# A statically scheduled transformer block: value weights by row blocks, one tile's layernorm sums on ScalarE, an earlier MLP weight load, a refitted cost model and a new ordering rule

## The chip, the cores and the metric

One core of a Trainium2 chip. The metric is the device time of one execution in microseconds (us). Each kernel is run several times; most runs of one kernel agree within 0.3%, and where they don't I say so. A profile records one execution; its span, from the first to the last instruction, is some 1.7 us shorter than the time.

PE is the matmul engine (TensorE), PEld its weight loads, DVE is VectorE, ACT is ScalarE, POOL is GpSimd, SP is SyncE. SP issues nearly all DMAs here, in order. A DMA *lands* when its completion is signalled; an engine *evicts* a result when it copies it out of PSUM. All runs here but one are in the fast state (granted clock 0.994 to 1.0); the slow one is e12's profiled run.

## The reference

Layernorm of x, then two branches that read the same normalised x, added to x. Shapes: S = 2048 rows, D = 640, 32 heads of 20, F = 1536, bf16.

```python
xn = layernorm(x)
q, k, v = split_heads(xn @ wqkv)
phi = lambda t: concat(softmax(t @ w_phi), softmax(-(t @ w_phi)))   # 20 -> 40 features per head
kv, z = phi(k)^T @ v, sum_s phi(k)
attn = (phi(q) @ kv) / (phi(q) @ z + 1e-6) @ wo
glu  = (silu(xn @ w1) * (xn @ w3)) @ w2
out  = x + attn + glu
```

## The kernel before

The rows are 16 tiles of 128. The program is not written in its final order. It is a set of *streams* (layernorms, transposes, keys and values, queries, MLP, output, ...). At build time, a list scheduler picks the next step again and again, with a cost model that guesses when each engine and each DMA will be done. The order it finds is fixed into the program; at run time the engines only wait on semaphores. A change of one guessed latency can therefore reorder everything after it.

The parts that matter here:

```python
# the cost model's DMA part (in commit); "T" marks a DMA that transposes
self.free[o.eng] = t + 0.45
if "T" == o.part:
    self.free[o.eng] = t + max(1.3, o.cost / 150e3)
self.bus = max(self.bus, t + 0.5) + o.cost / (280e3 if o.part else 305e3)
o.end = self.bus + (1.6 if t < 3.5 else 2.6)
# ... cut ...
def first_loads():
    load_x(0, 1)                      # and x tile 1 from ACT's queue
    for a in (0, 320):                # wv in two column halves
        P.dma("SP", wv[:, :, a:a + 320], wqkv_t[:, :, 2 * D + a:2 * D + a + 320])
        load_x(2 + a // 320, 3 + a // 320)
    w13(0, 512)                       # MLP columns 0-511 of w1 and w3
    # ... phi, wqkT for the keys, x tiles 4-11; columns 512-1023 only once xnT of tile 7 is issued
# ... cut ...
def ln_sums(t, q):                    # DVE: two of these per tile, then one aggregate
    P.op("DVE", "bn_stats", ...)
# ... cut: the choice of the next step, among all streams ...
if any(o.eng == "PE" for o in ops):
    at = max(P.ready(ops), P.free["PE"] + 0.15)
    if i == MLPS and P.free["DVE"] > P.free["PE"] + LAG:
        rank = n
# ... the smallest (at, rank) wins, so rank decides among steps that are ready
```

Names in the traces: `xnT` is the normalised x, transposed; `PS` is PSUM; `w_s` covers w1, w3 and w2; `wqkT` are the transposed query and key weights, which are multiplied ("folded") with the block-diagonal `BDc`; `eqt`/`EqT` are the query features of a tile and their transpose, made by a DMA; `KVc` is the kv state; `oT` is the attention output, transposed by a DMA as well.

The softmax here doesn't subtract the row's maximum and nothing guards it: scores larger than these inputs give would overflow.

Of the kernel before, what the change touches and what calls it, by code (L numbers as in the profile page):

```python
# [3 lines left out]
ACT = mybir.ActivationFunctionType  # L4
# [5 lines left out]
D = 640  # L10
# [33 lines left out]
class _Program:  # L44
# [123 lines left out]
    def commit(self, ops):  # L168
        for o in ops:
            o.idx = len(self.ops)  # L170
            o.deps = self.find_deps(o)
            t = self.free[o.eng]
            for d in o.deps:
                t = max(t, d.end + 0.07)
            o.start = t
            if o.dma:
                self.free[o.eng] = t + 0.45
                if "T" == o.part:
                    self.free[o.eng] = t + max(1.3, o.cost / 150e3)
                self.bus = max(self.bus, t + 0.5) + o.cost / (280e3 if o.part else 305e3)  # L180
                o.end = self.bus + (1.6 if t < 3.5 else 2.6)
            else:
                o.end = t + o.cost
                self.free[o.eng] = o.end
            self.ops.append(o)
            if o.eng == "POOL" and not o.dma:
                self.pool = o
            for g in o.reads:
                if isinstance(g, tuple):
                    self.bank.setdefault(g, {})[o.eng] = o  # L190
                else:
                    self.last_r.setdefault(g, {})[("dma", o.idx) if o.dma else o.eng] = o
            for g in o.writes:
                if isinstance(g, tuple):
                    self.bank.setdefault(g, {})[o.eng] = o
                else:
                    self.last_w[g] = o
                    self.last_r.pop(g, None)
# [45 lines left out]
def bass_parallel_sum__linear_kernel_hedgehog__glu_gated_swiglu__prompt_kernel(  # L244
# [10 lines left out]
):  # L255
    bf = DT.bfloat16
    LAG = 4.0
    AHEAD = 2
    PACE = 2.2
    f32 = DT.float32  # L260
# [25 lines left out]
    rstd = new("rstd", [128, T, 8], f32)  # L286
    mhalf = new("mhalf", [128, 4], f32)
    warm = new("warm", [128, 8], f32)
    g_s = new("g_s", [128, 2, H], f32)
    FM = new("FM", [128, 6, 3], bf)  # L290
    S64 = new("S64", [128, 3, 72], f32)
# [114 lines left out]
    def load_x(a, b):  # L406
        P.dma("SP", x_tok[:, a:b, :], x_t[:, a:b, :])

    def first_loads():
        load_x(0, 1)  # L410
        o = P.dma("ACT", x_tok[:, 1:2, :], x_t[:, 1:2, :])
        o.reads = P.regions(zero[:])
        for a in (0, 320):
            P.dma("SP", wv[:, :, a:a + 320], wqkv_t[:, :, 2 * D + a:2 * D + a + 320])
            load_x(2 + a // 320, 3 + a // 320)
        w13(0, 512)
        P.dma("SP", phi_s[:], phi_t)
        P.dma("SP", wqkT[:, DC:2 * DC, :], A_wqkv[:, D:2 * D], True)
        load_x(4, 8)
        load_x(8, 12)  # L420


    def consts():
# [21 lines left out]
    def ln_rstd(t0, n):  # L445
        for t in range(t0, t0 + n):
            o, i = mv[:, t, 0:2], bst[:, t, 0:15]
            P.op("DVE", "bn_aggr", [o], [i], (o, i), cost=0.15)
        m, v, r, z = mv[:, t0:t0 + n, 0], mv[:, t0:t0 + n, 1], rstd[:, t0:t0 + n, 0], rstd[:, t0:t0 + n, 1]
        P.op("POOL", "tensor_tensor", [r], [v, mhalf[:, 0:n]], (r, v, mhalf[:, 0:n], ALU.pow),  # L450
             cost=0.6)
        if t0 >= 4:
            P.op("POOL", "tensor_scalar_mul", [z], [m], (z, m, -1.0), cost=0.25)
            P.op("POOL", "tensor_tensor", [z], [z, r], (z, z, r, ALU.mult), cost=0.25)

    def ln_stats(t0, n):
        for t in range(t0, t0 + n):
# [50 lines left out]
    def proj(t, w, k):  # L508
        for q in range(2):
            for i in range(DC):  # L510
                mm(bank(k + q, 320), xnT[:, i, t * 128:(t + 1) * 128],
                   w[:, i, 320 * q:320 * q + 320], i == 0, i == DC - 1)

    def v_half(t, q, k):
        for i in range(DC):
            mm(bank(k, 320), xnT[:, i, t * 128:(t + 1) * 128], wv[:, i, 320 * q:320 * q + 320],
               i == 0, i == DC - 1)
        evac(v2[:, t, 336 * q:336 * q + 336].rearrange("p (h c) -> p h c", c=21)[:, :, 0:DH],
             bank(k, 320).rearrange("p (h c) -> p h c", c=DH))

    def v_tile(t, k):
        proj(t, wv, k)
# [29 lines left out]
    def normalise(e, c, n):  # L552
        s, r = S64[:, nnorm[0] % 3, 0:c * n], rS64[:, nnorm[0] % 3, 0:c * n]
        nnorm[0] += 1
        P.op("DVE", "tensor_reduce", [s], [e], (s, e, AX.X, ALU.add), cost=0.12 + free(e) / 960)
        P.op("DVE", "reciprocal", [r], [s], (r, s), cost=0.65)
        r = r.rearrange("p (c n) -> p c n", n=n)
        for a, b in ((0, c // 2), (c // 2, c)):
            ev = e[:, a:b, :, :]
            tt("POOL", ev, ev, r[:, a:b, :].unsqueeze(3).to_broadcast([128, b - a, n, DH]), ALU.mult)  # L560
# [89 lines left out]

    def norms():
        yield lambda: (memset("DVE", zero[:], 0.0), memset("DVE", warm[:], 0.0), first_loads(), consts())
        for t in range(4):
            yield lambda t=t: ln_sums(t, 0)
            if t == 1:
                for c, lo, hi in ((1, 0, 256), (2, 256, D)):
                    yield lambda lo=lo, hi=hi: ln_apply(0, lo, hi)
                    done["first"] = c
                done["ln"] = 1
            elif t:  # L660
                yield lambda t=t: ln_apply(t - 1)
                done["ln"] = t
            yield lambda t=t: (ln_sums(t, 1), ln_rstd(t, 1))
        yield lambda: ln_apply(3)
        done["ln"] = 4
        yield block_diag
        todo = []
        for t in range(4, T + 2, 2):
            if t == T or t > done["k"] + 8 or t == 12 and done["w"] < 8:
                for u in todo:  # L670
                    yield lambda u=u: ln_apply(u)
                    done["ln"] = u + 1
                todo = []
            if t == T:
                break
            while t > done["k"] + 8 or t == 12 and done["w"] < 8:
                yield None
            yield lambda t=t: ln_stats(t, 2)
            for u in todo:
                yield lambda u=u: ln_apply(u)  # L680
                done["ln"] = u + 1
            todo = [t, t + 1]
        yield consts_late
# [3 lines left out]
            yield lambda dc=dc: fold_mm(1, dc, banks(2))  # L687
        done["f"] += 1

    done["w"] = 4  # L690

    def k_norms():
        for t in range(T):
# [54 lines left out]
    def loads():  # L748
        while done["t"] < 4:
            yield None  # L750
        for t in range(4, T):
            while done["ln"] <= t:
                yield None
            yield lambda t=t: P.dma("SP", xnT[:, :, t * 128:(t + 1) * 128], x_tok[:, t, :], True)
            done["t"] = t + 1
            if t == 7:
                yield lambda: (w13(512, 1024), load_x(12, 16))
                done["w"] = 8
            if t == 9:
                yield lambda: w13(1024, 1536)  # L760
                done["w"] = 12
                yield lambda: P.dma("SP", wqkT[:, 0:DC, :], A_wqkv[:, 0:D], True)
                done["f"] = 2

    def attention():
# [4 lines left out]
        for t in range(4):  # L770
            while done["t"] <= t:
                yield None
            for q in range(2):
                yield lambda t=t, q=q: v_half(t, q, banks(1))
        while done["f"] < 1:
# [44 lines left out]
    def outs():  # L820
        for t in range(T):
            while done["o"] <= t or done["h"] <= t // 4:
# [2 lines left out]

    streams = [norms(), transposes(), fold_k(), attention(), k_norms(), loads(), queries(), q_norms(),
               q_transposes(), o_transposes(), mlps(), outs()]
    MLPS = 10
    URGENT = {0: 4.0, 4: 4.0, 7: 4.0, 8: 4.0, 9: 4.0}
    n = len(streams)  # L830
    heads, alive = [None] * n, [True] * n
    while any(alive):
        best = None
        for i in range(n):
            if heads[i] is None and alive[i]:
                s = next(streams[i], StopIteration)
                if s is StopIteration:
                    alive[i] = False
                else:
                    heads[i] = s  # L840
            if heads[i] is None:
                continue
            save = nmlp[0], nnorm[0], len(finish)
            ops = P.step(heads[i])
            after = nmlp[0], nnorm[0], finish[save[2]:]
            nmlp[0], nnorm[0] = save[:2]
            del finish[save[2]:]
            rank = i
            if any(o.eng == "PE" for o in ops):
                at = max(P.ready(ops), P.free["PE"] + 0.15)  # L850
                if i == MLPS and P.free["DVE"] > P.free["PE"] + LAG:
                    rank = n
            else:
                at = P.start_of(ops[0])
                if i in URGENT:
                    now, mine = P.free["PE"], P.free[ops[0].eng]
                    if at <= max(now, mine) + 0.3 and at < now + URGENT[i]:
                        at = now + 0.1 - URGENT[i]
            if best is None or (round(at, 2), rank) < best[:2]:
                best = (round(at, 2), rank, i, ops, after)  # L860
# [69 lines left out]
```

## Time and profile before

272.03 us median of three runs (271.89 to 272.31). From the page of the profile (busy time and share of the span by engine, then busy tenths in 40 slices of the span, then the chain that ended last):

```profile
span 270.6 us, 4817 instructions
PE 264.2 (98%) x1951; PEld 162.6 (60%) x1951; DVE 184.0 (68%) x308; ACT 101.9 (38%) x218; POOL 99.3 (37%) x108
...
PE   8899989999999999999999999999999999999996
...
DMA  7981799850000396463856636150726300031211
...
PE 86%; ACT 6%; DMA 5%; SPq 2%; issue 0%; DVE 0%
```

PE is busy nearly all the time, and nearly all of that is work at full rate. So the ceiling for any change that removes no matmul is the time that PE waits. I cut the span into three segments: the start (up to the first MLP matmul), the middle (from there to the first matmul of the kv sum), and the late part (to the end of PE's work: kv, queries, output). From the view of stretches; the columns are the stretch, its length, the busy time of PE, PEld, DVE, ACT and POOL, the granted clock, the DMA share and GB/s:

```profile
0.00:14.50 14.50, 12.21 (x75) 6.61 (x76) 7.75 (x22) 5.66 (x12) 6.00 (x21) 1.00 0.99 252
14.50:85.75 71.25, 69.89 (x472) 43.14 (x470) 61.01 (x99) 49.13 (x75) 51.26 (x55) 1.00 0.50 116
85.75:268.27 182.52, 182.05 (x1407) 112.80 (x1405) 114.93 (x188) 47.15 (x131) 42.08 (x33) 1.00 0.40 86
...
20.00:25.00 5.00, 5.00 (x36) 3.42 (x35) 4.86 (x14) 3.13 (x5) 2.25 (x6) 1.00 0.00 0
```

The middle has 1.36 us without PE work, the start 2.3 us, the late part 0.5 us. The last line shows the stretch in which the DMA queue does nothing. PE's timeline of the start (start, duration, engine, operation, output<-inputs, shapes, count, and in brackets the idle time before and what ended it):

```profile
6.41 1.09 PE L102 MATMUL PS<-wv,xnT 128*128 128x320 bf16 x5
7.93 0.85 PE L102 MATMUL PS<-wv,xnT 128*128 128x320 bf16 x5 [0.43 <-DMA wv<-in_A_wqkv_dram]
8.62 0.44 PE L102 MATMUL PS<-ident,x_tok 128*128 128x128 bf16 x5
9.58 0.96 PE L102 MATMUL PS<-wv,xnT 128*128 128x320 bf16 x5 [0.53 <-ACT xnT L102]
...
12.10 0.44 PE L102 MATMUL PS<-ident,x_tok 128*128 128x128 bf16 x5
12.38 2.28 PE L102 MATMUL PS<-wv,xnT 128*128 128x320 bf16 x15
...
14.50 2.32 PE L102 MATMUL PS<-xnT,w_s 128*128 128x512 bf16 x10
```

`ident,x_tok` are the five transposes of a tile, `wv,xnT` its values. And of the middle, the two places where PE waits:

```profile
40.02 1.52 PE L102 MATMUL PS<-Wkp,xnT 128*128 128x320 bf16 x10 [0.70 <-DMA xnT<-x_tok]
...
48.42 0.47 PE L102 MATMUL PS<-BDc,wqkT 128*128 128x140 bf16 x6 [0.65 <-DMA wqkT<-in_A_wqkv_dram]
```

A bracket gives idle time after a modelled end of the matmul before. The start-to-start excess over the matmul's own rate is larger: 0.87 and 0.82 us. I use the latter below for PE's waits.

### The profile page before, as it was taken

How to read it: one execution, taken by the hardware profiler on the slowest of the kernel's cores; microseconds unless marked ns; L12 is line 12 of the kernel's file. 1: busy time of each engine (PE TensorE's matmuls, PEld its weight loads, DVE VectorE, ACT ScalarE, POOL GpSimd, SP SyncE). 2: the span in 40 equal slices, each digit the busy share in tenths (PEclk: the TensorE clock that was granted, in tenths of full speed). 3: DMA queues.
4: the chain of work that ended last, by engine and by line, in shares of the span. 5: the costliest groups of instructions: out<-in, count | busy, mean ns of one | idle time of the engine just before them, and what ended most of it. 6: DMA issues, size and time to landing. Idle time of an engine off the chain costs nothing.

```text
span 270.6 us, 4817 instructions
## 1 busy us (share of the span) xinstructions
PE 264.2 (98%) x1951; PEld 162.6 (60%) x1951; DVE 184.0 (68%) x308; ACT 101.9 (38%) x218; POOL 99.3 (37%) x108
## 2 busy tenths in 40 slices
PE   8899989999999999999999999999999999999996
PEld 3556666577446846476756565657564444677773
DVE  4569689799896399959779766749577766311112
ACT  3467997687431455405233224043312222000000
POOL 3314288689998082704555221303330000000000
PEclk9999999999999999999999999999999999999999
DMA  7981799850000396463856636150726300031211
GB/s 209 288 235 24 185 269 290 107 150 2 0 0 2 105 290 129 59 126 65 173 78 145 140 66 126 27 126 0 127 57 126 51 0 0 0 94 54 81 43 48
DMA packets 63366, 27.73 MB, mean 102 GB/s; under 512 B 49904, under 2 KB 63344, under 8 KB 63344
## 3 DMA queue, kind: packets, MB, share of 16 engines
q1 hardware_dynamic: 63200, 27.26, 44.9%
q8 instruction: 15, 0.25, 0.4%
q10 hardware_dynamic: 144, 0.16, 0.2%
q14 instruction: 7, 0.06, 0.1%
HBM read 12.81 MB, written 2.62 MB: 57 GB/s over the span
## 4 chain that ended last, share of the span: by engine, by line
PE 86%; ACT 6%; DMA 5%; SPq 2%; issue 0%; DVE 0%
PE PS L102 86%; DMA wqkT<-in_A_wqkv_dram 3%; ACT ekt L102 3%; DMA wv<-in_A_wqkv_dram 2%; SPq L114 2%; ACT x_tok L102 1%; ACT v L102 1%; ACT eqt L102 0%; ACT th L102 0%; DVE xres L102 0%; ACT xnT L102 0%
## 5 line engine op out<-in xcount | busy, mean ns | idle before, releaser
L102 PE MATMUL PS<-xnT,w_s 128*128 128x512 bf16 x480 | 107.0, 379 | 0.5 <-ACT eqt L102 0.5
L102 PEld LDWEIGHTS PS<-xnT,w_s 128*128 128x128 bf16 x480 | 46.4, 98 | 53.4 <-ACT eqt L102 0.8
L102 POOL TENSOR_TENSOR eqt<-eqt,rS 128x600 bf16<-128x600 bf16 (+1 forms) x32 | 40.9, 1305 | 75.5 <-DVE rS L102 75.5
L102 ACT ACTIVATE th<-PS 128x512 f32<-128x512 f32 x48 | 28.7, 597 | 75.6 <-PE PS L102 75.6
L102 PE MATMUL PS<-w_s,hT 128*128 128x320 bf16 (+2 forms) x384 | 54.9, 299 | 0.0
L102 DVE SCALAR_TENSOR_TENSOR t<-th,PS 128x512 bf16<-128x512 f32 x48 | 32.4, 676 | 29.6 <-ACT th L102 29.6
L102 PEld LDWEIGHTS PS<-w_s,hT 128*128 128x128 bf16 x384 | 37.1, 98 | 15.1
L102 POOL TENSOR_TENSOR ekt<-ekt,rS 128x640 bf16<-128x640 bf16 x32 | 39.6, 1274 | 8.4 <-DVE rS L102 8.4
L102 ACT ACTIVATE eqt<-PS 128x240 bf16<-128x240 f32 (+1 forms) x96 | 26.7, 348 | 35.0 <-PE PS L102 34.5
L102 DVE TENSOR_TENSOR xres<-PS,xres 128x640 bf16<-128x640 f32 (+2 forms) x17 | 13.4, 786 | 37.2 <-PE PS L102 37.1
L102 DVE SCALAR_TENSOR_TENSOR hT<-t,PS 128x512 bf16<-128x512 bf16 x48 | 33.0, 687 | 1.7
L102 PE MATMUL PS<-wv,xnT 128*128 128x320 bf16 x160 | 25.0, 299 | 1.1 <-ACT xnT L102 0.5
L102 DVE TENSOR_REDUCE S<-eqt 128x66 f32<-128x1320 bf16 x16 | 24.1, 1509 | 2.6 <-ACT eqt L102 2.6
L102 ACT ACTIVATE ekt<-PS 128x640 bf16<-128x640 f32 x32 | 22.3, 702 | 8.6 <-PE PS L102 8.0
L102 PE MATMUL PS<-Wkp,xnT 128*128 128x320 bf16 x160 | 23.9, 299 | 0.7 <-DMA xnT<-x_tok 0.7
L102 PE MATMUL PS<-wo_s,oT 128*128 128x320 bf16 (+2 forms) x160 | 24.5, 299 | 0.0
L102 PE MATMUL PS<-Wqp,xnT 128*128 128x360 bf16 (+1 forms) x160 | 23.7, 299 | 0.0
L102 DVE TENSOR_REDUCE S<-ekt 128x64 f32<-128x1280 bf16 x16 | 23.1, 1447 | 0.0
L102 PEld LDWEIGHTS PS<-wv,xnT 128*128 128x128 bf16 x160 | 15.0, 98 | 8.3 <-ACT xnT L102 1.7
L102 PEld LDWEIGHTS PS<-Wkp,xnT 128*128 128x128 bf16 x160 | 15.4, 98 | 7.2 <-ACT ekt L102 1.0
L102 PEld LDWEIGHTS PS<-Wqp,xnT 128*128 128x128 bf16 x160 | 15.2, 98 | 6.8
L102 PEld LDWEIGHTS PS<-wo_s,oT 128*128 128x128 bf16 x160 | 15.1, 98 | 6.4
(48 smaller groups left out, 157.1 us busy)
## 6 DMA issues: line engine op xcount, KB each, us to landing
w_s<-in_B_w_dram SPq DMA_DIRECT2D x6, 640.0 KB, 6.7
xres<-in_A_x_dram SPq DMA_DIRECT2D x16, 160.0 KB, 2.5
out_dram<-xres SPq DMA_DIRECT2D x15, 160.0 KB, 1.9
x_tok<-in_A_x_dram SPq DMA_DIRECT2D x3, 640.0 KB, 6.4
w_s<-in_B_w_dram SPq DMA_DIRECT2D x1, 1920.0 KB, 8.5
wv<-in_A_wqkv_dram SPq DMA_DIRECT2D x2, 400.0 KB, 4.9
wo_s<-in_A_wo_dram SPq DMA_DIRECT2D x1, 800.0 KB, 4.9
x_tok<-in_A_x_dram SPq DMA_DIRECT2D x3, 160.0 KB, 4.3
```

The source lines that it names most:

```text
L102: o = _Op(eng, lambda: m(*args, **kw), r, w, cost)
L114: o = _Op(eng, lambda: m(out, in_), self.regions(in_), self.regions(out), nbytes, True)
```

## The change

The intent: fill the idle stretches of PE. wv comes in row blocks, so that tile 0 can begin on the first rows and use both column halves; the sums of layernorm tile 1 are made by ACT's accumulators while DVE does tile 0; MLP columns 512-1023 are loaded in the idle stretch of the DMA queue instead of in front of x of tiles 12-15; keys yield to MLP blocks when ACT is behind; and the cost model is fitted to measured latencies. The core of the diff:

```diff
+                turn = "T" == o.part
+                self.free[o.eng] = t + (max(1.28, o.cost / 120e3) if turn else 0.46)
+                rate = (280e3 if o.cost < 300e3 else 235e3) if turn else 330e3 if t < 4.5 else 285e3
+                self.bus = max(self.bus, t + 0.5) + o.cost / rate
+                o.end = self.bus + (1.6 if turn else 1.5 if t < 4.5 else 1.9)
 ... (replaces the five lines shown above)
-        for a in (0, 320):
-            P.dma("SP", wv[:, :, a:a + 320], wqkv_t[:, :, 2 * D + a:2 * D + a + 320])
-            load_x(2 + a // 320, 3 + a // 320)
+        for t, a, b in ((2, 0, 2), (3, 2, DC)):
+            P.dma("SP", wv[:, a:b, :], wqkv_t[:, a:b, 2 * D:3 * D])
+            load_x(t, t + 1)
 ...
         load_x(8, 12)
+        w13(512, 1024)
 ...
+    def act_sums(t):
+        i = x_tok[:, t, :]
+        for f, c in ((ACT.Copy, 0), (ACT.Square, 1)):
+            a = sums[:, c, 0:1]
+            P.op("ACT", "activation", [xres[:, c, :], a], [i], (xres[:, c, :], i, f), dict(accum_out=a), ...)
 ... (mean and variance from the sums by four small DVE operations; the power on POOL as before)
+            if t == 0:
+                for lo, hi in ((0, 3), (3, 4), (4, DC)):
+                    yield lambda lo=lo, hi=hi: v_first(0, lo, hi)
+                continue
 ...
-                yield lambda: (w13(512, 1024), load_x(12, 16))
-                done["w"] = 8
+                yield lambda: load_x(12, 16)
 ...
+                if i == ATTN and not done["kv"] and P.free["ACT"] > P.free["PE"] + ALAG:    # ALAG = 3.0
+                    rank = n + 1
 ... (layernorms run 7 instead of 8 tiles ahead of the keys; eight MLP blocks are at hand from the beginning; the guessed cost of a reciprocal on DVE falls from 0.65 to 0.56 us)
```

More of the change, by code (lines that the diff above doesn't have):

```diff
@@ L176, in commit @@
             if o.dma:
-                self.free[o.eng] = t + 0.45
-                if "T" == o.part:
-                    self.free[o.eng] = t + max(1.3, o.cost / 150e3)
-                self.bus = max(self.bus, t + 0.5) + o.cost / (280e3 if o.part else 305e3)
-                o.end = self.bus + (1.6 if t < 3.5 else 2.6)
+                turn = "T" == o.part
[3 more added lines that the diff above has]
+                o.end = self.bus + (1.6 if turn else 1.5 if t < 4.5 else 1.9)
             else:
@@ L257, in bass_parallel_sum__linear_kernel_hedgehog__glu_gated_swiglu__prompt_kernel @@
     LAG = 4.0
+    ALAG = 3.0
+    LEAD = 7
     AHEAD = 2
@@ L288, in bass_parallel_sum__linear_kernel_hedgehog__glu_gated_swiglu__prompt_kernel @@
     warm = new("warm", [128, 8], f32)
+    sums = new("sums", [128, 4, 8], f32)
     g_s = new("g_s", [128, 2, H], f32)
@@ L454, in ln_rstd, with small, act_mean, act_rstd @@
             P.op("POOL", "tensor_tensor", [z], [z, r], (z, z, r, ALU.mult), cost=0.25)
+    def act_sums(t):
+        i = x_tok[:, t, :]
+        for f, c in ((ACT.Copy, 0), (ACT.Square, 1)):
+            a = sums[:, c, 0:1]
+            P.op("ACT", "activation", [xres[:, c, :], a], [i], (xres[:, c, :], i, f), dict(accum_out=a),
+                 cost=0.2 + D / 960)
+    def small(o, i, a, f, b=None, g=None):
+        r = [x for x in (i, a, b) if hasattr(x, "ap")]
+        P.op("DVE", "tensor_scalar", [o], r, (o, i, a, b, f) + (() if g is None else (g,)), cost=0.13)
+    def act_mean(t):
+        m, n, q = mv[:, t, 0:1], sums[:, 2, 0:1], sums[:, 3, 0:1]
+        small(m, sums[:, 0, 0:1], 1.0 / D, ALU.mult)
+        small(n, sums[:, 0, 0:1], -1.0 / D, ALU.mult)
+        small(q, n, m, ALU.mult, EPS, ALU.add)
+    def act_rstd(t):
+        v, r = mv[:, t, 1:2], rstd[:, t, 0:1]
+        small(v, sums[:, 1, 0:1], 1.0 / D, ALU.mult, sums[:, 3, 0:1], ALU.add)
+        P.op("POOL", "tensor_tensor", [r], [v, mhalf[:, 0:1]], (r, v, mhalf[:, 0:1], ALU.pow), cost=0.6)
     def ln_stats(t0, n):
@@ L512, in proj, with v_out @@
                    w[:, i, 320 * q:320 * q + 320], i == 0, i == DC - 1)
+    def v_out(t, q, k):
+        evac(v2[:, t, 336 * q:336 * q + 336].rearrange("p (h c) -> p h c", c=21)[:, :, 0:DH],
+             bank(k, 320).rearrange("p (h c) -> p h c", c=DH))
     def v_half(t, q, k):
@@ L517, in v_half, with v_first @@
                i == 0, i == DC - 1)
-        evac(v2[:, t, 336 * q:336 * q + 336].rearrange("p (h c) -> p h c", c=21)[:, :, 0:DH],
-             bank(k, 320).rearrange("p (h c) -> p h c", c=DH))
+        v_out(t, q, k)
+    def v_first(k, lo, hi):
+        for i in range(lo, hi):
+            for q in range(2):
+                mm(bank(k + q, 320), xnT[:, i, 0:128], wv[:, i, 320 * q:320 * q + 320], i == 0, i == DC - 1)
+        if hi == DC:
+            v_out(0, 0, k)
+            v_out(0, 1, k + 1)
     def v_tile(t, k):
@@ L555, in normalise @@
         P.op("DVE", "tensor_reduce", [s], [e], (s, e, AX.X, ALU.add), cost=0.12 + free(e) / 960)
-        P.op("DVE", "reciprocal", [r], [s], (r, s), cost=0.65)
+        P.op("DVE", "reciprocal", [r], [s], (r, s), cost=0.56)
         r = r.rearrange("p (c n) -> p c n", n=n)
@@ L652, in norms @@
         yield lambda: (memset("DVE", zero[:], 0.0), memset("DVE", warm[:], 0.0), first_loads(), consts())
-        for t in range(4):
-            yield lambda t=t: ln_sums(t, 0)
-            if t == 1:
-                for c, lo, hi in ((1, 0, 256), (2, 256, D)):
-                    yield lambda lo=lo, hi=hi: ln_apply(0, lo, hi)
-                    done["first"] = c
-                done["ln"] = 1
-            elif t:
-                yield lambda t=t: ln_apply(t - 1)
-                done["ln"] = t
+        yield lambda: act_sums(1)
+        yield lambda: ln_stats(0, 1)
+        yield lambda: act_mean(1)
+        for c, lo, hi in ((1, 0, 256), (2, 256, D)):
+            yield lambda lo=lo, hi=hi: ln_apply(0, lo, hi)
+            done["first"] = c
+        done["ln"] = 1
+        yield lambda: act_rstd(1)
+        for t in range(2, 4):
+            yield lambda t=t: ln_sums(t, 0)
+            yield lambda t=t: ln_apply(t - 1)
+            done["ln"] = t
             yield lambda t=t: (ln_sums(t, 1), ln_rstd(t, 1))
@@ L668, in norms @@
         for t in range(4, T + 2, 2):
-            if t == T or t > done["k"] + 8 or t == 12 and done["w"] < 8:
+            if t == T or t > done["k"] + LEAD or t == 12 and done["t"] < 8:
                 for u in todo:
@@ L675, in norms @@
                 break
-            while t > done["k"] + 8 or t == 12 and done["w"] < 8:
+            while t > done["k"] + LEAD or t == 12 and done["t"] < 8:
                 yield None
@@ L688, in fold_k @@
         done["f"] += 1
-    done["w"] = 4
+    done["w"] = 8
     def k_norms():
@@ L827, in bass_parallel_sum__linear_kernel_hedgehog__glu_gated_swiglu__prompt_kernel @@
                q_transposes(), o_transposes(), mlps(), outs()]
-    MLPS = 10
+    MLPS, ATTN = 10, 3
     URGENT = {0: 4.0, 4: 4.0, 7: 4.0, 8: 4.0, 9: 4.0}
```

## The prediction

> **What bounds it now.** TensorE. The page gives PE busy 264.2 of 270.6 us (98%), DVE 68%, ACT 38%; the chain that ended last is 86% PE. In the PE timeline the 480 MLP matmuls of 512 columns start 217.5 ns apart, the 320-column ones 136 ns. The Trainium skill ("TensorE: Matmul & The Clock Gate", section "Wait — 56ns, not 53.3ns?") gives N / 2.4 GHz + about 2.5 ns, 215.8 and 135.8: the trace agrees, so nearly the whole span is at the engine's floor, and no matmul is removed. Start-to-start excesses over 60 ns sum to 7.0 us, 1.7 of it the half-rate warm-up. Recoverable are about 5.3 us:
>
> 1. Start, 5.1 to 13 us: 2.7 us. PE waits 0.43 us for the second wv half (landed 7.88), 0.53 for xnT of tile 1, and works in pieces; v of tiles 0-3 ends at 14.5.
> 2. 39.0 us: 0.87 us. xnT of tile 8, issued at 31.5 behind two w loads and x 12-15 (issued 29.7 to 30.9), landed at 39.88.
> 3. 47.4 us: 0.82 us. Transposed wqkT landed at 48.29, same queue. (0.64 us at 110.7 us, on ACT eqt, is not addressed.)
>
> Even a perfect result is near 266.7 us, 1.95% better.
>
> **What the change does.**
> - wv by rows: same bytes and place in the queue, rows of 1280 B instead of 640. All of wv should land where the second half does, 7.4 to 7.8 us; tile 0 starts with two row blocks. Small gain.
> - ACT sums for tile 1: a 640-wide eviction took 0.70 us, so I estimate 0.7 to 0.85 us for each of two. x tile 1 landed at 3.56 and ACT is idle until 5.97, so they end about 5.3. DVE loses two bn_stats (0.5 us each) and an aggregate (0.22) and gains four small operations (estimate 0.1 us each). Tile 1's apply moves from 7.1 to about 6.6, tile 3's from 11.3 to about 10.2; v of tiles 0-3 should end at 12.8 to 13.5: 1.0 to 1.7 us gained. The first MLP needs w3, landed at 12.08, so it can use this.
> - MLP columns 512-1023: 1.3 MB move from 29.7 us, where they delay tile 8, into 20 to 25 us, where the DMA share is 0.00. At about 300 GB/s they fit just before the xnT transposes of 24.5 us. Later loads land several us earlier; stalls 2 and 3 should go: 1.7 us.
> - Eight instead of four MLP chunks are available early, and keys yield when ACT lags over 3 us (ACT is fully busy from 25 to 40 us). This moves work; I count no gain beyond stall 2.
> - The altered cost model reorders everything statically. I allow 0.2 to 0.5 us of new stalls.
>
> **Sum.** 1.4 + 1.7 - 0.2 = 2.9 us, all on PE, the critical path: about 269.1; I say 269.0 us, 267.5 to 271.0. Faster by over 2% (under 266.6) 0.04, within 2% 0.94, slower by over 2% 0.02.
>
> **What would show it.** PE busy stays near 263 to 264 us while span falls to about 267.6. v of tile 3 ends before 13.5 us; no 0.4 us wait on wv; two 640-wide ACT activations between 3.6 and 5.4 us; w columns 512-1023 issued near 14 us, landed before 25; no PE wait on xnT<-x_tok near 39 us nor on wqkT near 48 us; from 68 us on all merely shifted.
>
> **What would make it wrong.** A second activation table load for Square (the first took 1.28 us); the accumulating activations running into tile 0's evictions; DVE's small operations waiting on ACT and holding back tile 0's apply; the early w load delaying the first xnT transposes and so the keys; new stalls from the reordered keys, queries and MLPs, which could eat the whole gain.

## The result, and the profile after

270.76 us median (270.69 to 270.91, four runs), before 272.17 us in all runs together; the ratio is 0.9949, with a 95% interval of 0.9932 to 0.9967. A ratio is the mean time of one kernel's fast runs over that of the other's fast runs of the same rounds, so it is not quite the ratio of the medians. So the change gained 1.4 us where I had forecast 3.0: the right direction and inside the range, but less than half the size.

```profile
span 269.0 us, 4811 instructions
PE 263.8 (98%) x1951; PEld 162.6 (60%) x1951; DVE 183.2 (68%) x305; ACT 107.0 (40%) x226; POOL 99.6 (37%) x108
...
PE   7999999999999999999999999999999999999996
...
DMA  7995798241000683844727325164206142011211
...
PE 93%; DMA 4%; ACT 1%; SPq 1%; DVE 0%; issue 0%
```

The same three segments:

```profile
0.00:13.67 13.67, 11.85 (x76) 6.63 (x76) 7.28 (x23) 7.00 (x16) 5.54 (x20) 1.00 0.95 254
13.67:83.28 69.61, 69.60 (x473) 43.26 (x470) 60.20 (x95) 52.59 (x79) 50.65 (x57) 1.00 0.51 121
83.28:266.67 183.39, 182.38 (x1407) 112.76 (x1405) 115.44 (x188) 47.40 (x131) 43.43 (x33) 1.00 0.38 85
```

Against before, the start is 0.83 us shorter, the middle 1.64 us shorter (PE is busy for all of it now), and the late part is **0.87 us longer**. The sum, 1.60 us, is the difference of the two spans. Both traces have 130 MLP matmuls ahead of the kv sum, so the segments hold the same work.

The start:

```profile
6.46 0.97 PE L102 MATMUL PS<-wv,xnT 128*128 128x320 bf16 x4 [0.20 <-ACT xnT L102]
7.72 0.45 PE L102 MATMUL PS<-wv,xnT 128*128 128x320 bf16 x2 [0.30 <-DMA wv<-in_A_wqkv_dram]
8.01 0.44 PE L102 MATMUL PS<-ident,x_tok 128*128 128x128 bf16 x5
8.28 1.43 PE L102 MATMUL PS<-wv,xnT 128*128 128x320 bf16 x9
...
11.27 0.44 PE L102 MATMUL PS<-ident,x_tok 128*128 128x128 bf16 x5
11.55 2.28 PE L102 MATMUL PS<-wv,xnT 128*128 128x320 bf16 x15
...
13.67 2.32 PE L102 MATMUL PS<-xnT,w_s 128*128 128x512 bf16 x10
```

After 7.72 us PE hardly pauses; before that it does little. The transposes of tile 1 (8.01) stand *behind* the two matmuls that wait for the second row block, although their input was ready at 7.07. The two lines that waited in the middle have no counterpart any more. The late part, where it lost time:

```profile
175.13 2.32 PE L102 MATMUL PS<-xnT,w_s 128*128 128x512 bf16 x10
177.85 0.51 PE L102 MATMUL PS<-KVc,EqT 128*128 128x63 bf16 x11 [0.40 <-DMA EqT<-eqt]
```

PE waits there 0.57 us (start to start) for a transposed query tile, a wait that before did not have. A second new one of 0.30 us stands before the MLP block at 104.78. PE's own line names nothing there, but that of its weight loads does, ACT's eviction of query features:

```profile
104.78 1.84 PEld L102 LDWEIGHTS PS<-xnT,w_s 128*128 128x128 bf16 x10 [0.25 <-ACT eqt L102]
```

So the late part's 0.87 us are 0.57 for a transpose and 0.30 for ACT. Another wait on ACT eqt, of 0.64 us, is in both kernels (110.7 us before, 108.5 after).

### The profile page after: what moved, and what is told of

It reads as the page before. It is cut to its first block, busy times and chain, and to the rows that moved or that the text cites. A ratio compares the mean times of both kernels' runs of the same rounds, so it can differ in the third digit from the quotient of the medians.

```text
span 269.0 us, 4811 instructions
## 1 busy us (share of the span) xinstructions
PE 263.8 (98%) x1951; PEld 162.6 (60%) x1951; DVE 183.2 (68%) x305; ACT 107.0 (40%) x226; POOL 99.6 (37%) x108
## 3 DMA queue, kind: packets, MB, share of 16 engines
q1 hardware_dynamic: 62560, 27.26, 43.5%
## 4 chain that ended last, share of the span: by engine, by line
PE 93%; DMA 4%; ACT 1%; SPq 1%; DVE 0%; issue 0%
PE PS L102 93%; DMA wv<-in_A_wqkv_dram 2%; DMA EqT<-eqt 2%; ACT eqt L102 1%; SPq L114 1%; DVE xres L102 0%
## 5 line engine op out<-in xcount | busy, mean ns | idle before, releaser
L102 PE MATMUL PS<-xnT,w_s 128*128 128x512 bf16 x480 | 108.2, 379 | 0.6 <-ACT eqt L102 0.5
L102 DVE TENSOR_TENSOR xres<-PS,xres 128x640 bf16<-128x640 f32 (+2 forms) x17 | 13.4, 786 | 33.1 <-PE PS L102 33.1
L102 DVE RECIPROCAL rS<-S 128x64 f32<-128x64 f32 (+1 forms) x32 | 17.9, 560 | 1.1
```

What stands on the lines that cost most here:

```text
L102: o = _Op(eng, lambda: m(*args, **kw), r, w, cost)
```

## The experiments

Fifteen runs (e15 is the changed kernel again), all of them correct. Where it helps I give "first MLP" (the end of the start) and "late part" as defined above. The kernels of one group ran on the same chip, with the kernel before beside them: e1 to e4, e5 to e8, e9 to e12, e13 to e15.

### What bounds the start: e1 to e4

**e1_split2**: tile 0's values are cut where the row blocks are.

```diff
-                for lo, hi in ((0, 3), (3, 4), (4, DC)):
+                for lo, hi in ((0, 2), (2, DC)):
```

> The changed kernel, but tile 0's v is issued in the pieces i=0..1 and i=2..4 (as the two wv row blocks arrive) instead of i=0..2, 3, 4; the order of PE's instructions is the same otherwise. My theory: in the changed kernel the start is bound by the landing of wv's second block (7.68 us) and by the PE work that is left then (about 5.7 us), because the transposes of tile 1 stand behind two matmuls that wait for that block. Here they move into the wait: v of tiles 0-3 ends at 13.4 us instead of 13.67, time 0.2 to 0.3 us shorter than the changed kernel (0.993 to 0.994 of before). Rival (the layernorm chain of tiles 2 and 3 bounds the start): v still ends at 13.6 to 13.7 us, time unchanged (0.995).

Measured: 270.16 us (0.9930). First MLP at 13.20 us. PE's timeline of e1:

```profile
6.85 0.58 PE L102 MATMUL PS<-wv,xnT 128*128 128x320 bf16 x3 [0.16 <-ACT xnT L102]
7.27 0.44 PE L102 MATMUL PS<-ident,x_tok 128*128 128x128 bf16 x5
7.58 1.67 PE L102 MATMUL PS<-wv,xnT 128*128 128x320 bf16 x11
```

The transposes moved into the wait, and the start shrank by 0.47 us, more than the 0.27 I expected; 0.14 of it is wv's second block, which landed at 7.53 us in this profile and at 7.68 in the changed kernel's. So in the changed kernel the start was bound by the order in front of the second block's landing, and not by the layernorms of tiles 2 and 3.

**e2_blk3**: three row blocks (0-1, 2-3, 4), with the values cut in the same way.

> As e1, but wv in three row blocks (0-1, 2-3, 4), so that only the last chunk's two matmuls of tile 0 wait for the last landing. My theory (landing of wv plus work left): v ends at 13.1 to 13.3 us, where tile 3's layernorm takes over as the bound. Rival (layernorm chain): 13.6 us as in the changed kernel. Rival 2 (the additional DMA costs queue time): wv lands 0.3 us or more later and v ends later than in e1.

Measured: 270.45 us (0.9932), first MLP at 13.20 us, in the expected band, but no better than e1: no PE wait on wv is left in either, so a finer cut has nothing to remove.

**e3_no_rows**: column halves of wv as before, all else as changed (the two hunks on wv and on tile 0 undone).

> The changed kernel with wv in column halves as before (v of tile 0 in halves), all else kept. My theory: the row blocks bring nothing, since the halves let PE do five matmuls and tile 1's transposes before the second half lands near 7.8 us: v ends at 13.3 to 13.7 us, not later than the changed kernel's 13.67. Rival (the intent of the change: row blocks are what shortened the start): v ends at 14.0 us or later.

Measured: 272.61 us (1.0015), first MLP at 14.30 us. My expectation was wrong by 0.6 us. wv landed at 7.34 us and wasn't the cause: PE waited 0.80 us (by the bracket) before 12.93 for ACT to evict tile 3's transposes, because the order that the scheduler found left no value matmuls to do meanwhile. So the row blocks helped in this schedule, and I can't separate the blocks from the order they led to. The late part was 184.92 us, with three PE waits on EqT of 0.63, 1.08 and 0.39 us: the first sign that such waits come and go with any edit.

**e4_no_act_sums**: tile 1's statistics on DVE again, row blocks kept.

```diff
-        yield lambda: act_sums(1)
         yield lambda: ln_stats(0, 1)
-        yield lambda: act_mean(1)
+        yield lambda: ln_sums(1, 0)
 ...
-        yield lambda: act_rstd(1)
+        yield lambda: (ln_sums(1, 1), ln_rstd(1, 1))
```

> The changed kernel with tile 1's statistics on DVE as before, row blocks kept. My theory: the statistics on ACT are what brought the 0.83 us at the start, by moving tile 3's normalisation from 11.27 to 10.44 us; without them tile 3's apply is back near 11.2 us and v ends at 14.2 to 14.5 us. Rival (row blocks brought it): v ends at 13.7 to 13.9 us.

Measured: 271.26 us (0.9967), first MLP at 14.85 us. The ACT sums are worth 1.2 us at the start when the row blocks are there. Together: neither 14.50 (the kernel before), row blocks only 14.85, ACT sums only 14.30, both 13.67, both and e1's cut 13.20. The two parts do little or harm alone and pay together, with the caveat that each edit also changed the order, and that the first of these five has the old cost model as well.

A second caveat is chance. The second part of wv lands at 7.34 to 7.88 us with column halves (before, e3, e10, e13) and at 6.88 to 7.90 with row blocks (the other twelve usable profiles), and at 7.35, 7.59, 7.65 and 7.68 us where the start is the same program (e9, e15, e11 and the changed kernel). In these four the first MLP comes 5.95 us after the first value matmul behind that landing, whenever it is. The same interval is 6.57 us in the kernel before (and in e10 and e13), 6.90 in e4, 6.75 in e3 and 5.62 in e1 (and in e14). So of the 0.83 us at the start some 0.6 belong to the change and 0.2 to an earlier landing; of e1's 0.47 us, 0.33 belong to its cut; and the ACT sums, with the row blocks, are worth 0.95 us rather than 1.2.

### What stalls the late part: e5 to e7, e11

In every trace so far, some EqT transposes took 3.5 to 4.1 us from issue to landing, and a few 4.3 to 5.4 us. The packets in the trace showed what the slow ones share: a packet of an *instruction* queue during the transfer, for ten of the eighteen over 4.1 us one of 16,384 bytes and about 1 us, for the others one of 8,192 bytes of a second such queue. Of the large ones the page counts 15 of these a run on one queue (`q8 instruction: 15, 0.25, 0.4%`), one per about 125 matmuls. The Trainium skill ("Runtime: NRT & Kernel Launch", section "Instruction fetch mechanics") says that an engine's instructions are refilled in 16 KiB blocks of 256 instructions by the sequencer's own DMA queue; 125 matmuls with their weight loads are about 250, so I take these for PE's; e5 and e6, which add PE instructions alone, move them. The page calls the cost "mostly hidden".

**e5_fetch12** and **e6_fetch24** shift those fetches without touching the order: the warm-up, which multiplies zeros, gets more and shorter matmuls with the same number of columns.

```diff
-        for n, rep in ((4, 8), (1, 7)):
+        for n, rep in ((4, 4), (1, 23)):      # e5: 12 matmuls more;  e6: ((1, 39),), 24 more
```

> The changed kernel with its warm-up cut into 27 matmuls instead of 15 (4 of 512 and 23 of 128 columns, the same number of columns), so that the program of every engine is in the same order, and only the PE's instruction stream is 12 matmuls longer. In all six traces so far, every EqT transpose that took over 4.1 us from issue to landing overlapped a packet of the instruction queue (16 KB, about 1 us; 15 of them a run), and those without took 3.5 to 4.1 us. My theory: the 0.57 us stall of PE at 177 us (and so about half of the gain that is missing late) is such a collision, at 175.0 us. With 12 matmuls more ahead, the fetch comes about 2 to 3 us earlier than the transpose issued at 173 us, whose landing falls to 3.6 us; the stall goes and the time is 0.5 to 0.6 us shorter than the changed kernel's (0.993 of before). Rival (the queue's own order, the store of the output and the transpose of oT beside it, delays this transpose): landing stays at 4.7 us and the stall at 0.5 us.

Measured: 270.97 us (0.9949). The time is of no use: its runs spread from 269.91 to 272.00, and in the profiled one the matmuls from 7 to 10 us start 266 ns apart instead of 135: PE ran at half rate there, and the first MLP came at about 15 us. That the new warm-up did this is not shown; e6, with a still finer one, has nothing of it. The late part can be read: 182.82 us, 0.57 less than the changed kernel's. The fetch began 0.9 us before the transpose was issued, the transpose took 3.94 us, and PE's timeline of e5 shows no wait:

```profile
176.41 2.32 PE L102 MATMUL PS<-xnT,w_s 128*128 128x512 bf16 x10
178.57 0.50 PE L102 MATMUL PS<-KVc,EqT 128*128 128x63 bf16 x11
```

> The same with 39 warm-up matmuls, 24 more. My theory: the fetches move on by another 2 to 3 us, so the transpose of 173 us stays at 3.6 us, and by counting matmuls the fetch of 157 us now falls into the transpose issued at 151.8 us (and that of 106.7 into the one of 101 us): it takes 4.6 to 5.3 us instead of 3.63, and PE waits up to 0.7 us near 156 us where it did not wait; time near the changed kernel's (0.995). Rival: as in e5, the stall stays at 177 us and none appears at 156.

Measured: 271.17 us (0.9963). The transpose of 173 us took 3.66 us. The fetch came at 153.6 us into the transpose issued at 152.3, which took 4.36 us where it had taken 3.63, and PE waited 0.17 us at 156.6, less than the 0.7 allowed. The transpose at 101.5 us took 3.81 us with a fetch 3.06 us after its issue, so that part missed. And one hit I had not foreseen: a fetch at 14.0 us delayed the transposing load of wqkT from 14.92 to 16.24 us, and PE waited for it, 1.17 us start to start.

The order of the data queue is the same in the changed kernel, e5 and e6; only the phase of the instruction stream differs, and the slow transposes move with it. So the queue's order is not the cause. Over 16 profiles (my own count from the packets and landings of the traces; e12 left out, see below):

```
EqT transposes, issue to landing       count   median (range), us    longest packet of the data queue meanwhile, median
no instruction packet overlaps          186    3.61 (3.48 to 4.07)   0.11 us
PE fetch begins 0.9-3.4 us after issue   24    5.03 (3.57 to 6.22)   1.55 us
```

(I chose the window of 0.9 to 3.4 us from these same data. Two of the 24 stayed fast, both with a fetch over 3 us after issue; 18 with a PE fetch at other times had a median of 3.84, range 3.58 to 4.80, and 28 that met only an 8 KB fetch of another queue one of 4.21, up to 4.67.) The Trainium skill ("DMA: Bandwidth & Descriptors", section "Queues, rings and completion order") says that each DMA engine switches between queues only after a whole packet. That would fit: one of the 16 engines is held for about 1 us, the transpose's packets on it wait, and the transpose lands when the last of its packets is through. This is an inference: the trace doesn't say which engine a packet ran on. The runs show the long packet and the late landing.

**e7_late11** tells the scheduler the truth about this one transpose: it assumes that the twelfth EqT lands 0.9 us later.

```diff
+                if o.name.startswith("dma:EqT"):
+                    self.turns += 1
+                    o.end += 0.9 if self.turns == 12 else 0.0
```

> The changed kernel, its scheduling model told that the twelfth EqT transpose lands 0.9 us later than it assumed; the order is the same up to there, and then an MLP column block goes ahead of the query block that stalled at 177 us. My theory: the schedule had no slack where the transpose was late; PE does other work meanwhile, the stall of 0.57 us goes although the transpose still takes 4.7 us, time 0.993 to 0.994 of before unless a later transpose is hit. Rival (the order makes the landing late): the wait appears elsewhere with the same size.

Measured: 270.30 us (0.9933; runs 270.17 to 271.41). The transpose still took 4.59 us; PE did an MLP block first and did not wait. Late part 182.82 us, as in e5: the 182.52 of before and the 0.30 of ACT.

**e11_eqt_slack** gives all EqT transposes 0.8 us more in the model, about what the old model had: for one of 360 KB the old formula gives 0.5 + 1.29 + 2.6 = 4.39 us on an idle queue, the new one 0.5 + 1.53 + 1.6 = 3.63.

```diff
-                o.end = self.bus + (1.6 if turn else 1.5 if t < 4.5 else 1.9)
+                o.end = self.bus + ((2.4 if o.name.startswith("dma:EqT") else 1.6) if turn else ...)
```

> The changed kernel whose scheduling model adds 0.8 us to the landing of every EqT transpose (about 4.4 us from issue to landing, as the old model had it, instead of 3.6); the order is the same up to the queries. My theory: the new model's figure, which is the usual case, leaves no room for transposes that an instruction fetch delays to 4.6 to 5.4 us; with 0.8 us of room the waits of PE on EqT (0.57 us in the changed kernel, 2.5 us in e8, 2.4 us in e3) fall below 0.3 us in sum, though two or more transposes still take over 4.4 us; the late part (first kv matmul to the end of PE) takes 182.0 to 182.9 us instead of 183.4, and the time is 0.993 of before. Rival (room is worth nothing, as the order that it forces has waits of its own): late part 183.4 us or more.

Measured: 269.57 us (0.9929; one run of 271.3, at a granted clock of 0.994, among those of 269.5). One EqT took 5.95 us, and PE did not wait for it or for any other. The late part:

```profile
83.25:265.42 182.17, 182.03 (x1407) 112.93 (x1405) 115.05 (x188) 47.17 (x131) 43.39 (x33) 1.00 0.40 86
```

Only one EqT was over 4.1 us, not the two over 4.4 that I expected; otherwise the theory held. The 0.64 us wait on ACT eqt went too, which I had not predicted: it belonged to the order, not to the load. So of the 1.22 us by which this late part is shorter than the changed kernel's, 0.57 are the transpose and 0.64 this other wait.

### What removed the waits of the middle: e8 to e10, e13

**e8_late_w**: MLP columns 512-1023 load late again, everything else as changed.

```diff
         load_x(8, 12)
-        w13(512, 1024)
 ...
-                yield lambda: load_x(12, 16)
+                yield lambda: (w13(512, 1024), load_x(12, 16))
+                done["w"] = 8                     # and 4 instead of 8 to begin with
```

> The changed kernel with MLP columns 512-1023 loaded late again (with x of tiles 12-15, as before), all else kept. My theory: this load's move accounts for the two removed stalls near 39 and 47 us (1.7 us). With it undone, PE waits again 0.5 to 1.0 us for xnT of tile 8 or 9 and for wqkT, together 1.0 to 1.7 us between 30 and 55 us; time 0.999 to 1.001 of before. Rival (keys giving way to MLP removes them): PE finds other work, no stall over 0.3 us there, time as the changed kernel.

Measured: 272.28 us (0.9995). My theory fell. The time was as forecast, but for another reason: no wait over 0.3 us between 20 and 80 us, middle 69.33 us (some matmul records are missing from this trace, also that of the first MLP matmul), although wqkT landed at 47.12 us:

```profile
13.78:83.11 69.33, 69.12 (x466) 43.18 (x470) 60.80 (x95) 51.50 (x78) 50.74 (x56) 1.00 0.51 121
```

What cost the time were three late waits on EqT of 0.51, 0.78 and 1.24 us, at transposes that took 5.0 to 6.2 us, each with a fetch inside; late part 185.35 us.

**e9_no_yield**: the early load stays, the rule goes (ALAG = 1e9).

> The changed kernel without the rule that keys give way to MLP when ACT lags; the early w load stays. e8 has refuted my view that the load's move alone removed the two stalls of the middle (with the load late, none came back). What is left: either measure alone is enough, or the rule alone did it. If either is enough (my theory now): from the first MLP matmul to the first kv matmul at most 0.3 us more than the work, as in the changed kernel, no PE wait over 0.3 us between 20 and 80 us. If the rule alone did it (rival): waits of 1 to 2 us come back between 25 and 60 us. The late part can hold other stalls of 0 to 2 us, since fetches fall elsewhere; I read each segment from the trace.

Measured: 272.09 us (0.9998). The middle takes 72.08 us, 2.5 us more than in the changed kernel. From e9's stretches and its list of waits:

```profile
13.34:85.42 72.08, 69.83 (x473) 43.22 (x471) 61.15 (x100) 48.28 (x74) 51.91 (x57) 1.00 0.51 117
```

```profile
PE PS L102 <- DMA wqkT<-in_A_wqkv_dram: 2.2, 1, 2.2
```

The early load alone doesn't do it, and the rival was right. wqkT landed at 45.7 us, earlier than before (48.29), but PE wanted it at 43.5. The late part is 182.80 us, without a wait on EqT.

**e10_before_early_w**: the kernel before with only the early load (and the guards that go with it).

> The kernel before with nothing but the early load of MLP columns 512-1023 (and the conditions that belong to it). Either is enough (my theory): the waits of 0.87 us at 39 and 0.82 us at 47 us go, nothing over 0.3 us takes their place in the middle; the start stays at 14.5 us. Rival (the rule alone did it): the middle still waits 1 to 2 us. Time 0.994 of before in the first case if the late part doesn't change, 1.0 in the second.

Measured: 271.71 us (0.9987). Between the two: middle 70.49 us, that is 0.76 us better than before, with waits of 0.27, 0.29 and 0.38 us left. Its late part, under the old cost model, is 182.52 us as before, although seven of its EqT transposes took 4.27 to 5.54 us: PE waits for none of them.

**e13_before_yield**: the kernel before with only the rule, four lines (the one that names ATTN is left out here).

```diff
+    ALAG = 3.0
 ...
+                if i == ATTN and not done["kv"] and P.free["ACT"] > P.free["PE"] + ALAG:
+                    rank = n + 1
```

> The kernel before with nothing but the rule that keys give way to MLP when ACT lags by over 3 us. Theory (the rule alone removes the stalls of the middle, by putting MLP blocks ahead of keys and of the fold, so that PE needs xnT of tile 8 and wqkT later, not because these land earlier): the middle (first MLP matmul to first kv matmul, for 130 MLP matmuls in it) takes 69.5 to 70.0 us instead of 71.25, with no wait over 0.4 us between 25 and 60 us, though wqkT lands at 47 us or later. Rival (it needs eight MLP chunks at hand, so the early load or the conditions that came with it are needed too): 70.5 us or more.

Measured: 270.43 us (0.9932): the rule alone gives at least as much as the whole change (0.27 us of it, in the profile, is an earlier landing of wv).

```profile
14.23:85.94 71.71, 71.70 (x483) 44.27 (x481) 61.19 (x98) 52.28 (x79) 51.57 (x55) 1.00 0.51 115
85.94:266.30 180.36, 179.89 (x1397) 111.84 (x1395) 113.41 (x186) 46.64 (x130) 42.12 (x33) 1.00 0.38 87
```

There are 140 MLP matmuls in this middle instead of 130. Ten are 2.16 us (216 ns each), so for equal work the middle is 69.55 us and the late part 182.52. wqkT landed at 48.26 us and xnT of tile 8 at 39.94, as late as before (48.29 and 39.88). PE didn't wait, because MLP blocks stood in front of the fold, which came at 52.95 us instead of 48.42:

```profile
52.95 0.48 PE L102 MATMUL PS<-BDc,wqkT 128*128 128x140 bf16 x6
```

The rule made the demand later, not the supply earlier. And the late part, with the old cost model, is the 182.52 of before.

### Both mended: e12, e14, e15

**e12_split2_late11** joins e1 and e7.

> e1 and e7 together: tile 0's v cut at the row blocks, and the twelfth EqT transpose assumed 0.9 us later. If the two gains are independent (my theory): v ends at 13.2 us, late part 182.8 us, span 267.9 us, time 269.6 us or 0.991 of before, faster than both kernels by 1.0 us (0.4%) over the changed one. Rival: the fetches, whose times move with the order, hit other transposes, late part 183.3 us or more, time 270.2 us as e1.

Measured: 269.84 us (0.9915), as expected. The profile fell into a run of 464 us at a granted clock of 0.559; I draw nothing from its segments.

**e14_split2_eqt_slack** joins e1 and e11; **e15_after_again** is the changed kernel beside it.

> e1 and e11 together. Theory (start and query stalls are independent terms): first MLP at 13.2 us, late part 182.2 us, span 267.2 us, time 269.0 us, 0.989 of before and 0.6% shorter than the changed kernel beside it. Rival (fetches move and hit elsewhere): late part 182.8 us or more, time 269.6 us or more.

> The changed kernel, unaltered, as a control beside e14: 270.7 us, 0.995 of before; the wait at 177 us is there again (0.4 to 0.8 us), as the fetch meets the same transpose; first MLP at 13.5 to 13.8 us.

Measured: e14 269.13 us (268.98 to 269.37; 0.9885, interval 0.9871 to 0.9899). e15 271.05 us (270.68 to 272.59; 0.9966). So e14 beats the kernel before by 1.2% and the changed one by 0.8% (0.9885 over 0.9966). Its late part is 182.18 us, as e11's. Its start ended at 13.54 us instead of 13.20, because wv's second block landed at 7.87 us (7.53 in e1): the values that need it began at 7.92 instead of 7.58, the same 0.34 us later. (x of tile 2 was late as well, 6.59 against 6.28, and with it tile 1's transposes, but these stand in front of the landing.)

```profile
7.52 0.45 PE L102 MATMUL PS<-ident,x_tok 128*128 128x128 bf16 x5 [0.23 <-DVE x_tok L102]
7.92 1.53 PE L102 MATMUL PS<-wv,xnT 128*128 128x320 bf16 x10
```

e15 (its run of 272.59 had a granted clock of 0.994) has the wait at 177 us again, 0.84 us this time, with a fetch 1.3 us after the transpose's issue and 5.03 us to its landing.

## Why the prediction was wrong

The sum was: start −1.4, middle −1.7, new stalls +0.2, together −2.9 us, stated as 269.0 us. The profile of the changed kernel says −0.83, −1.64 and +0.87, together −1.60 (by time −1.4).

- **Bound and ceiling** (right). PE at 98%, no work removed, about 5.3 us to be had. (The 217.5 ns of the prediction is a mean that includes waits; within the blocks the MLP matmuls start 216 ns apart.) The best kernel found here (e14) gained about 3.1 us of it, 1.15% of 272.2.
- **The new stalls: the step that failed most.** "The altered cost model reorders everything statically. I allow 0.2 to 0.5 us of new stalls", of which 0.2 went into the sum; and "from 68 us on all merely shifted". It was 0.87 us: 0.57 for the EqT transpose at 177 us, 0.30 for ACT at 104.8. I took the fitted cost model for a mere reshuffle. Before, the model's 4.39 us for an EqT transpose was too long for the usual case (3.6 us), and this error was room: the kernel before has four transposes of 4.3 to 4.8 us and no PE wait on any. The new 3.63 us is the usual case, and an instruction fetch makes some take 4.3 to 6.2 us. e5 removed the 0.57 us wait by moving the fetch, e7 by telling the scheduler, e11 by giving back the room. The old formula bears it out: in the three profiles that have it (before, e10, e13), 13 of 48 EqT transposes took 4.27 to 5.54 us, and PE waited for none. With the new one and no room, the loss is a matter of where the fetches fall: none in e4 and e9, 0.57 and 0.84 us in the two profiles of the changed kernel, up to 2.5 us in e8.
- **The start: mis-sized.** "v of tiles 0-3 should end at 12.8 to 13.5: 1.0 to 1.7 us gained". It ended at 13.67, 0.83 us gained, some 0.6 of it by the change and the rest by an earlier landing of wv. The layernorms moved as I said (tile 1's apply at 6.62, tile 3's at 10.44, against about 6.6 and 10.2), and the ACT sums took 0.74 and 0.72 us, but I did not ask what PE had left to do when wv landed at 7.68: 36 value matmuls and 15 transposes, which are 36 × 0.1355 + 15 × 0.056 = 5.7 us, so 13.4 at best. And I overlooked that the piece i = 0..2 reaches into the second block and holds tile 1's transposes back. e1 got 0.33 us for that, apart from the landing.
- **The middle: right size, wrong cause.** "Later loads land several us earlier; stalls 2 and 3 should go: 1.7 us", and of the yielding rule "I count no gain beyond stall 2". The loads did land earlier (wqkT at 44.33 instead of 48.29), but e8 shows that the waits are gone without that, e9 that they come back without the rule, e13 that the rule alone is enough. The 1.7 us came out right for a reason that I had counted at nothing: luck.
- **The dangers named**: no second table load and no collision of the accumulating activations with tile 0's evictions; the early w load landed at 24.12 us and the xnT transposes were issued at 23.69, earlier than before (24.53). The last one named, "new stalls from the reordered keys, queries and MLPs", is what took the gain, for a cause that I did not know.

What stays open: whether row blocks have a worth of their own apart from the order they led to (e3), why the new order meets ACT's 0.30 us near 104.8 us, and what the other fitted costs, LEAD and the tile-12 guards do alone, which no run tried.

## What to carry to other kernels

When PE is saturated, cut the span at points that separate equal work, and compare segment by segment: a total of −1.4 us hid −0.83, −1.64 and +0.87. In a static order, a latency guess is not only an estimate but also the room for bad cases: in both kernels that got 0.8 us of it back (e11, e14), PE waited for no transpose, one of 5.95 us included. And when a wait for data vanishes, ask whether the data came earlier or the demand came later: here four lines of priority did what a moved load was meant to do.

## What the Trainium skill lacked or had wrong

- "Runtime: NRT & Kernel Launch", section "Instruction fetch mechanics", calls the cost of crossing a 16 KiB boundary "mostly hidden", and lacks what it costs the transfers beside it. In these runs a PE refill that began 0.9 to 3.4 us after the issue of a DMA transpose went with a median of 5.03 us to its landing, against 3.61 without one (24 and 186 transposes), and PE waited for such transposes 0.17 to 1.24 us where the order had no room.
- "DMA: Bandwidth & Descriptors" describes the switch between queues per packet, which the long packets fit, but has no size for a refill packet (about 1 us for 16,384 bytes here) and doesn't warn of it for transposes, whose longest packet went from 0.11 to 1.55 us (medians).
- The same page gives a DMA transpose a bandwidth, but no time from issue to landing: 3.6 us for 360 KB within SBUF here.
- "ScalarE: Activation LUTs", section "What ACT_TABLE_LOAD costs", gives 186 ns + 0.833 ns per element for immediate scale and bias, 719 ns for 640; 737 and 721 ns were measured, so it agrees. It mentions the accumulator output but not that reading it is a further instruction of 0.19 us (an ACTIVATION_READ_ACCUMULATOR in the trace), which the next activation overlapped by half.
